# x's block sums of a sparse attention and MoE kernel, cut into ten short steps and built one pass ahead

## The chip, the cores and the metric

The kernel runs on one core of one Trainium2 chip. The metric is the device time of one execution in microseconds (us); before the change it is 1703.1 us, the median of three runs (1699.97 to 1703.55). TensorE multiplies matrices (PE in the profile; its weight loads are PEld), VectorE (DVE) and ScalarE (ACT) do elementwise work, GpSimd (POOL) does elementwise work on SBUF alone, and SyncE (SP) issues all DMAs of this kernel. Each engine works through its own instructions in order; semaphores order the engines among each other.

## The reference

```
scores = q @ k^T / sqrt(64)                 # 4 batches, 8 heads, 576 tokens, 64 columns
heads 0-3: local mask (0 <= i-j < 32);  heads 4-7: strided mask (i >= j, i%32 == j%32)
attn = exp(scores - max) / (sum + 1e-9);    x = attn @ v  as [2304 tokens, 512]
P = exp(x @ w_gate - global max)            # 2304 x 8
8 times: P /= row sum + 1e-9;  P /= column sum + 1e-9;  P *= 2304/8
out = sum over 8 experts e of  P[:, e] * (relu(x @ w1[e]) @ w2[e])      # 512 -> 1024 -> 512
```

All of it is in fp32; every operand of the large products is split into a high part (fp32r, rounded by a copy on ACT) and a low part (source minus high part, a subtraction on POOL or DVE), and a product is three matmuls: high x high, high x low, low x high.

## The kernel before

**Stages.** First comes attention: 32 steps, the first nine ahead of everything else, the rest beside the first expert. Their output x, split in two, lies in `reg`, in five chunks of tokens (four of 512, one of 256), and is also stored to DRAM (`xd`). Second, expert 0 is computed plainly, in 56 *slots* (the loop at L733). A slot is `layer1` of one chunk and one of four blocks of 128 hidden columns (12 matmuls, then ReLU: high part on ACT, low part on DVE), and then `layer2` of the slot before it. The first 36 slots have nine chunks of 256 tokens (first half of the hidden columns, u = 0), the last 20 have the chunks 0, 512, 2048, 1024, 1536 (u = 1), four slots each; the one at 2048 has 256 tokens, the others 512. While attention lasts a slot also has an attention step; from slot 26 on attention is over, and the slots carry other work from generators, one step of each a slot (L754).

Third come experts 1 to 7 in three passes of 768 tokens, 28 groups a pass, 84 in all (the loop at L779). A group (`first`) is seven products of blocks in place of eight, as in Strassen's scheme: hidden blocks come from sums and differences of blocks of w1 (`prep_w1`: three POOL instructions, then four splits) and of x. Its second layer (`second`, six blocks of 12 matmuls) runs inside the next group, as `fill(0)` to `fill(5)`. DVE adds each block times its gate to `acc`.

**The block sums of x.** `build_s(p, k)` makes them for pass p and half k of 256 columns: four loads from `xd` (768 KB in all), on POOL one addition of high and low parts (128x1536) and four differences or sums (128x384), the split (ACT copies 128x1536, POOL subtracts), and two stores to `sd`. The three passes' six builds are one generator `sums()` with three steps a build: loads; POOL's sums; split and stores. All six run in the slots after attention. `st` and `so` have one buffer each.

**The gate.** `gating()` has 28 steps: five times logits and transposes, two for the global maximum, and for each of eight normalizations a row step on DVE (L342 to L347) and a column step (TensorE's sum over partitions with a matrix of ones, L350, then DVE, L352 to L354).

**The first group's operands.** `early()` loads w1 for group 0, prepares it ten slots later, loads w2 and the first three operands of x into `reg`, where chunks no longer needed lay; the other operands of x are loaded behind the slots (L763). After the slots the pools `w1` (four buffers of 4096 bytes a partition) and `h` (two of 4096) are closed, and in their place, in this order, `rab` (12288 bytes: raw w1 blocks and their differences), `u` (4608 bytes: m1, u2, u3) and `hg` are opened (L766). The last slot's layer 2, which reads `h`, runs as `fill(0)` of group 0, behind its first three products (`rest_of_plain`, L774).

**Scaling.** Expert 0's result in `acc` has to be multiplied by its gate before other experts are added. `scale(p)` (L770) does it for six tiles on DVE, in group 0 for the first pass, and behind the last but one group of a pass for the next one (L782).

Of the kernel before, what the change touches and what calls it, by code (L numbers as in the profile page):

```python
# [8 lines left out]
F32 = mybir.dt.float32  # L9
F32R = mybir.dt.float32r  # L10
# [41 lines left out]
def kernel(  # L52
# [9 lines left out]
    nc = tc.nc  # L62
# [91 lines left out]
    def split(hi, lo, src):  # L154
        nc.scalar.activation(hi, src, AF.Copy)  # L155
        nc.gpsimd.tensor_tensor(lo, src, hi.bitcast(F32), op=ALU.subtract)  # L156
# [296 lines left out]
    def build_s(p, k):  # L453

        st = pools["sb"].tile([P, 4, 2, TN], F32, tag="sx", name=f"sx_{p}_{k}", bufs=1)
        t0 = 2 * TN * p
        for i, (dh, th) in enumerate(((0, 0), (0, 1), (1, 1), (1, 0))):
            nc.sync.dma_start(  # L458
                st[:, i], xd[:, :, k + 2 * dh, t0 + TN * th : t0 + TN * (th + 1)]
            )  # L460
        yield
        x, s = st[:, :, 0, :], st[:, :, 1, :]
        nc.gpsimd.tensor_tensor(x, x, s, op=ALU.add)  # L463
        x11, x21, x22, x12 = (x[:, i, :] for i in range(4))
        for i, (a, b, op) in enumerate((
            (x21, x22, ALU.add),
            (x21, x11, ALU.subtract),
            (s[:, 0, :], x11, ALU.subtract),
            (x12, s[:, 2, :], ALU.subtract),
        )):  # L470
            nc.gpsimd.tensor_tensor(s[:, i, :], a, b, op=op)  # L471
        yield
        so = pools["sb"].tile([P, 2, 4, TN], F32R, tag="so", name=f"so_{p}_{k}", bufs=1)
        split(so[:, 0], so[:, 1], s)
        for i in range(2):
            nc.sync.dma_start(sd[:, p, :, i, k, :], so[:, i].bitcast(F32))
        yield

    def load_x(p, name):
        if p >= NPASS:  # L480
            return
        o = xops[name].bitcast(F32)
        if name in SOPS:
            nc.sync.dma_start(o, sd[:, p, SOPS.index(name)])
        else:
            th, dh = int(name[1]) - 1, int(name[2]) - 1
            t0 = 2 * TN * p + TN * th
            nc.sync.dma_start(o, xd[:, :, 2 * dh : 2 * dh + 2, t0 : t0 + TN])

    def load_w1g(g):  # L490
        if g >= NG:
            return
        _, e, j = groups[g]
        pool, tag = (raw_p, "raw") if g == 0 else (pools["rab"], "rab")
        ra, rb = (
            pool.tile([P, 2, 2, P], F32, tag=tag, name=f"r{x}_{g}") for x in ("a", "b")
        )
        for t, i, dh, fh in ((ra, 0, 0, 0), (ra, 1, 1, 1), (rb, 0, 0, 1), (rb, 1, 1, 0)):
            f0 = (FP * fh + j) * P
            nc.sync.dma_start(  # L500
                t[:, i],
                w1[e, 2 * P * dh : 2 * P * (dh + 1), f0 : f0 + P].rearrange("(k p) f -> p k f", p=P),
            )
        wraw[g] = ra, rb

    def load_w2g(g):
        if g >= NG:
            return
        _, e, j = groups[g]
        w2raw[g] = [raw_p.tile([P, D], F32, tag="raw", name=f"r2_{g}_{i}") for i in range(2)]  # L510
        for i in range(2):
            load_w2(w2raw[g][i], e, (FP * i + j) * P)

    def prep_w1(g):

        if g >= NG:
            return
        ra, rb = wraw.pop(g)
        w = wops[g % 2]
        pool, tag = (raw_p, "raw") if g == 0 else (pools["rab"], "rtu")  # L520
        rt, ru = (
            pool.tile([P, 2, 2, P], F32, tag=tag, name=f"r{x}_{g}", bufs=None if g == 0 else 2)
            for x in ("t", "u")
        )
        fl = "p i k f -> p i (k f)"
        a, b, t, u = (x.rearrange(fl) for x in (ra, rb, rt, ru))
        nc.gpsimd.tensor_tensor(  # L527
            t, b[:, 0:1, :].to_broadcast([P, 2, 2 * P]), a, op=ALU.subtract
        )
        nc.gpsimd.tensor_tensor(u[:, 0], a[:, 1], t[:, 0], op=ALU.subtract)  # L530
        nc.gpsimd.tensor_tensor(u[:, 1], b[:, 1], u[:, 0], op=ALU.subtract)
        split(w[:, 0, 0:2], w[:, 1, 0:2], ra)
        yield
        split(w[:, 0, 4:6], w[:, 1, 4:6], ru)
        yield
        split(w[:, 0, 2:4], w[:, 1, 2:4], rt)
        yield
        split(w[:, 0, 6], w[:, 1, 6], rb[:, 1])
        yield
# [121 lines left out]
    def attention_scores():  # L661
        if at_k < NS:
            at_scores(at_k)
# [39 lines left out]
            op=ALU.subtract,  # L703
        )

    def sums():
        for p in range(NPASS):
            for k in range(2):
                yield from build_s(p, k)

    def early():

        load_w1g(0)
        for _ in range(9):
            yield
        yield from prep_w1(0)
        load_w2g(0)
        for name in XOPS[:3]:
            load_x(0, name)

    slots = []
    for u in range(UPE):
# [7 lines left out]
                slots.append((u, c, ft, ci == len(chunks) - 1))  # L730
    bg = []
    prev = None
    for u, c, ft, last in slots:  # L733
        layer1(u, c, ft)
        if last and u + 1 < UPE:
            split_w(u + 1, ft, 0)
        busy = at_k < NS + LAG
        if busy:
            attention_values()
            attention_scores()  # L740
        if prev is not None:
            pu, pc, pft, plast = prev
            layer2(pu, pc, pft)
            if plast and pu + 1 < UPE:
                split_w(pu + 1, pft, 1)
        if busy:
            attention_rest()
            if at_k == NS + LAG:
                store_x()
                stacks["right"].close()  # L750
                pools["sb"] = ctx.enter_context(tc.tile_pool(name="sb", bufs=1, side="right"))
                bg = [gating(), sums()]
        else:
            for x in bg:  # L754
                next(x, None)
            if u == 1 and c[0] == 0 and ft == 0:
                bg.append(early())
        prev = (u, c, ft, last)
    for x in bg:
        for _ in x:  # L760
            pass

    for name in XOPS[3:]:  # L763
        load_x(0, name)
    stacks["left"].close()
    for name, bufs in (("rab", 4), ("u", 1), ("hg", 8)):  # L766
        pools[name] = ctx.enter_context(tc.tile_pool(name=name, bufs=bufs, side="left"))
    load_w1g(1)

    def scale(p):  # L770
        for t in range(6 * p, 6 * (p + 1)):
            nc.vector.tensor_scalar_mul(acc[:, t, :], acc[:, t, :], gate[:, t, 0:1])  # L772

    def rest_of_plain(i):  # L774
        if i == 0:
            layer2(*prev[:3])
            scale(0)

    for g in range(NG):  # L779
        p, e, j = groups[g]  # L780
        first(g, (lambda i: second(g - 1, i)) if g else rest_of_plain)
        if p + 1 < NPASS and e == E - 1 and j == FP - 2:  # L782
            scale(p + 1)
    for i in range(6):
        second(NG - 1, i)

# [78 lines left out]
```

## Time and profile before

| | |
|---|---|
| median of three runs | 1703.1 us (1699.97 to 1703.55) |
| the profiled execution | 1701.88 us, span of its instructions 1699.8 us |
| TensorE busy | 1633.4 us (96%), mean granted clock 0.982 |
| DVE, ACT, POOL busy | 942.0 us (55%), 586.9 us (35%), 958.4 us (56%) |
| TensorE's share of the chain that ended last | 86%; POOL 4%, DMA 3%, DVE 2%, issue 2% |
| DMA | 160.57 MB, mean 94 GB/s |

The profile is of one execution. Busy time counts compute instructions only. The granted clock is TensorE's, as a share of its full 2.4 GHz; a mean below 1 says that the engine ran for part of the stretch at its lower level, 1.2 GHz. The chain that ended last is followed back from the last instruction, at each step to what released it. In a list by time a row has its start, its length, engine, line, operation, what it writes and reads, sizes and a count of merged instructions; in brackets stands how long the engine had been idle before it, and what ended that. A row of matmuls ends with the modelled end of the last, a little behind the start of the next row, so the distance from start to start is what a set of matmuls takes.

### The profile page before, as it was taken

Reading aid. Unit: us, or ns where it says so; the run is one execution under the profiler, and the core shown is the slowest. Engines: PE = TensorE matmul, PEld = TensorE weight load, DVE = VectorE, ACT = ScalarE, POOL = GpSimd, SP = SyncE. Lnnn points to the kernel's source line nnn. Section 1 sums busy time; section 2 is a strip of 40 time slices with the busy share of each in tenths; the row PEclk is TensorE's granted clock in tenths of the full one; section 3 lists DMA queues with packets and bytes.
Section 4 is the critical chain, followed back from the end, with each engine's and each line's share of the span. In section 5 each row is a group of like instructions: output and inputs, shape, how many; then the busy total and the mean of one; then the engine's idle time right before and its main releaser. Section 6 shows DMA issues by size and latency. Waiting matters only on the chain.

```text
span 1699.8 us, 23976 instructions
## 1 busy us (share of the span) xinstructions
PE 1633.4 (96%) x8779; PEld 1446.0 (85%) x8779; DVE 942.0 (55%) x1914; ACT 586.9 (35%) x1386; POOL 958.4 (56%) x862
## 2 busy tenths in 40 slices
PE   6999678889999999999999999999999999999999
PEld 5888556678998998998999899899989989989997
DVE  4664113445566556557556555655665655565565
ACT  6664121113333333333333333333333333333332
POOL 4221464316666665665666666566666666656663
PEclk9999888899999999999999999999999999999999
DMA  6553445422222222224421222222162122222211
GB/s 206 176 165 139 142 164 161 155 69 75 68 57 75 72 64 64 75 69 149 149 69 56 75 72 61 67 75 69 56 242 69 56 75 69 62 68 75 68 51 50
DMA packets 158101, 160.57 MB, mean 94 GB/s; under 512 B 11168, under 2 KB 122272, under 8 KB 157984
## 3 DMA queue, kind: packets, MB, share of 16 engines
q1 hardware_dynamic: 157984, 159.05, 29.7%
q8 instruction: 69, 1.13, 0.3%
q14 instruction: 48, 0.39, 0.1%
HBM read 135.41 MB, written 23.59 MB: 94 GB/s over the span
## 4 chain that ended last, share of the span: by engine, by line
PE 86%; POOL 4%; DMA 3%; DVE 2%; issue 2%; SPq 1%; ACT 1%; POOLq 0%; ACTq 0%; DVEq 0%
PE yg L572 40%; PE bb L555 15%; PE ba L555 10%; PE bc L555 10%; PE y L404 4%; PE ph L380 4%; DMA sx<-xd 2%; POOL sx L471 1%; POOL sx L463 1%; SPq L458 1%; POOL so L156 1%; DVE acc L772 1%; PE tp L257 1%; PE sc L197 1%; PE pv L270 1%
## 5 line engine op out<-in xcount | busy, mean ns | idle before, releaser
L572 PE MATMUL yg<-w2g,h 128*128 128x512 f32 x3024 | 755.8, 394 | 1.4 <-POOL w2g L156 1.2
L572 PEld LDWEIGHTS yg<-w2g,h 128*128 128x128 f32 x3024 | 564.2, 188 | 105.8 <-POOL w2g L156 3.6
L577 DVE SCALAR_TENSOR_TENSOR acc<-yg,gate,acc 128x512 f32<-128x512 f32 x504 | 377.8, 750 | 246.5 <-PE yg L572 246.5
L555 PE MATMUL bb<-reg 128*128 128x384 f32 x1512 | 307.3, 338 | 6.1 <-DVE u L608 6.1
L555 PEld LDWEIGHTS bb<-reg 128*128 128x128 f32 x1512 | 272.0, 188 | 21.8 <-DVE u L608 7.3
L156 POOL TENSOR_TENSOR reg<-rt,reg 128x512 fp32r<-128x512 f32 x84 | 109.1, 1298 | 239.4 <-ACT reg L155 239.4
L156 POOL TENSOR_TENSOR reg<-ru,reg 128x512 fp32r<-128x512 f32 x84 | 120.8, 1438 | 204.1 <-ACT reg L155 199.2
L156 POOL TENSOR_TENSOR w2g<-r,w2g 128x512 fp32r<-128x512 f32 x168 | 217.5, 1295 | 11.2 <-ACT w2g L155 11.2
L555 PE MATMUL ba<-reg 128*128 128x384 f32 x1008 | 205.8, 339 | 0.6 <-ACT m L621 0.6
L555 PE MATMUL bc<-reg 128*128 128x384 f32 x1008 | 203.1, 335 | 0.6 <-POOL reg L156 0.6
L555 PEld LDWEIGHTS ba<-reg 128*128 128x128 f32 x1008 | 182.1, 188 | 15.0 <-ACT m L621 1.0
L611 ACT ACTIVATE h<-u 128x384 fp32r<-128x384 f32 x168 | 88.3, 526 | 270.6 <-DVE u L608 270.6
L555 PEld LDWEIGHTS bc<-reg 128*128 128x128 f32 x1008 | 178.0, 189 | 0.9 <-POOL reg L156 0.9
L608 DVE TENSOR_TENSOR u<-bb,m 128x384 f32<-128x384 f32 x168 | 93.6, 557 | 147.6 <-PE bb L555 137.9
L404 PE MATMUL y<-w,h 128*128 128x512 f32 x432 | 122.3, 428 | 39.7 <-ACT h L386 25.5
L611 ACT ACTIVATE h<-ba 128x384 fp32r<-128x384 f32 x84 | 41.3, 492 | 337.3 <-PE ba L555 337.3
L404 PEld LDWEIGHTS y<-w,h 128*128 128x128 f32 x432 | 84.7, 204 | 61.7 <-ACT h L386 33.6
L527 POOL TENSOR_TENSOR rt<-rb,ra 128x512 f32<-128x512 f32 x84 | 109.3, 1301 | 37.4 <-DMA rb<-in_w 37.4
L156 POOL TENSOR_TENSOR reg<-ra,reg 128x512 fp32r<-128x512 f32 x84 | 108.9, 1296 | 35.6 <-ACT reg L155 35.5
L380 PE MATMUL ph<-reg,w 128*128 128x256 f32 (+1 forms) x672 | 118.4, 327 | 0.0
L608 DVE TENSOR_TENSOR u<-bc,u 128x384 f32<-128x384 f32 x168 | 93.7, 558 | 44.3 <-PE bc L555 41.4
L611 ACT ACTIVATE h<-m 128x384 fp32r<-128x384 f32 x84 | 44.0, 524 | 184.2 <-DVE m L608 184.2
(77 smaller groups left out, 1488.9 us busy)
## 6 DMA issues: line engine op xcount, KB each, us to landing
r<-in_w SPq DMA_DIRECT2D x168, 256.0 KB, 3.1
ra<-in_w SPq DMA_DIRECT2D x168, 128.0 KB, 2.3
rb<-in_w SPq DMA_DIRECT2D x168, 128.0 KB, 2.3
sx<-xd SPq DMA_DIRECT2D x24, 384.0 KB, 5.9
sd<-so SPq DMA_DIRECT2D x12, 768.0 KB, 3.9
reg<-sd SPq DMA_DIRECT2D x12, 768.0 KB, 8.9
xd<-reg SPq DMA_DIRECT2D x4, 2048.0 KB, 8.0
reg<-xd SPq DMA_DIRECT2D x9, 768.0 KB, 8.3
```

The lines of the kernel that those rows point to most:

```text
L156: nc.gpsimd.tensor_tensor(lo, src, hi.bitcast(F32), op=ALU.subtract)
L197: nc.tensor.matmul(sc[QT * j : QT * j + QT, i, :], t[sl, q0 : q0 + QT], t[sl, k0 : k0 + KW], start=True, stop=True,)
L257: nc.tensor.transpose(tp[:nk, i, :rows], sm[:, i0 + i, :], ident[:rows, :rows])
L270: nc.tensor.matmul(pv[DH * j : DH * j + DH, i * QT : (i + 1) * QT], tv[:nk, i, j, :], pt[:nk, i, QT * j : QT * j + QT], start=True, stop=True,
L380: nc.tensor.matmul(ph[:, :n], w[:, i, dt, :], xv(x, dt, c0, n), start=(k == 0), stop=(k == 3 * NDT - 1),)
L404: nc.tensor.matmul(y, h[:, a, i * P : (i + 1) * P], w[:, b, :], start=(ft == 0 and first), stop=(ft == FH - 1 and a == 1),)
L527: nc.gpsimd.tensor_tensor(t, b[:, 0:1, :].to_broadcast([P, 2, 2 * P]), a, op=ALU.subtract)
L555: nc.tensor.matmul(out[:, :TN], w[:, i, k, :], xops[x][:, xi, k, :], start=(start and n == 0), stop=(n == 5), skip_group_check=True,)
L572: nc.tensor.matmul(y, hv[f][:, a, o : o + P], w2s[g][f][:, b, :], start=(n == 0), stop=(n == 5))
L577: nc.vector.scalar_tensor_tensor(acc[:, t, :], y, gate[:, t, e : e + 1], acc[:, t, :], op0=ALU.mult, op1=ALU.add)
L608: nc.vector.tensor_tensor(o, bank, s, op=ALU.add)
L611: nc.scalar.activation(h[i][f][:, 0], src, AF.Relu)
```

## The change

A build is cut into ten steps: loads; the addition in two halves; the four differences in two pairs; an empty step; ACT's copy in two halves; POOL's subtraction in two halves; stores. `sums(p)` makes one pass only. Pass 0 is built in the slots after attention, one step a slot; the sums of pass p + 1 are built in the groups of pass p, one step behind each group. The gate's generator steps twice a slot, behind layer 1 and behind layer 2. `early()` is replaced by a list of work by slot (`beside_second_half`, counted from the first slot of u = 1) which also loads more operands of x and scales the first six tiles of `acc`; all scaling is on ACT, for the next pass two tiles behind each of the first three groups of expert 7. The pool `u` is opened ahead of `rab`.

```diff
--- before.py
+++ after.py
@@ -460,7 +460,11 @@
             )
         yield
         x, s = st[:, :, 0, :], st[:, :, 1, :]
-        nc.gpsimd.tensor_tensor(x, x, s, op=ALU.add)
+        for i in (0, 2):
+            nc.gpsimd.tensor_tensor(
+                x[:, i : i + 2], x[:, i : i + 2], s[:, i : i + 2], op=ALU.add
+            )
+            yield
         x11, x21, x22, x12 = (x[:, i, :] for i in range(4))
         for i, (a, b, op) in enumerate((
             (x21, x22, ALU.add),
@@ -469,9 +473,19 @@
             (x12, s[:, 2, :], ALU.subtract),
         )):
             nc.gpsimd.tensor_tensor(s[:, i, :], a, b, op=op)
-        yield
+            if i % 2:
+                yield
         so = pools["sb"].tile([P, 2, 4, TN], F32R, tag="so", name=f"so_{p}_{k}", bufs=1)
-        split(so[:, 0], so[:, 1], s)
+        yield
+        for i in (0, 2):
+            nc.scalar.activation(so[:, 0, i : i + 2], s[:, i : i + 2], AF.Copy)
+        yield
+        for i in (0, 2):
+            nc.gpsimd.tensor_tensor(
+                so[:, 1, i : i + 2], s[:, i : i + 2], so[:, 0, i : i + 2].bitcast(F32),
+                op=ALU.subtract,
+            )
+            yield
         for i in range(2):
             nc.sync.dma_start(sd[:, p, :, i, k, :], so[:, i].bitcast(F32))
         yield
@@ -703,20 +717,27 @@
             op=ALU.subtract,
         )
 
-    def sums():
-        for p in range(NPASS):
-            for k in range(2):
-                yield from build_s(p, k)
-
-    def early():
-
-        load_w1g(0)
-        for _ in range(9):
-            yield
-        yield from prep_w1(0)
-        load_w2g(0)
-        for name in XOPS[:3]:
-            load_x(0, name)
+    def sums(p):
+        for k in range(2):
+            yield from build_s(p, k)
+
+    def scale(t):
+        nc.scalar.activation(acc[:, t, :], acc[:, t, :], AF.Copy, scale=gate[:, t, 0:1])
+
+    def beside_second_half():
+
+        work = {i: [] for i in range(20)}
+        work[3].append(lambda: load_w1g(0))
+        work[10].append(lambda: load_x(0, "x11"))
+        for i, name in ((12, "s2"), (12, "s1"), (13, "x12"), (16, "s3"), (16, "x22")):
+            work[i].append(lambda name=name: load_x(0, name))
+        w = prep_w1(0)
+        for i in range(5):
+            work[9 + i].append(lambda: next(w, None))
+        work[14].append(lambda: load_w2g(0))
+        for i in range(6):
+            work[14 + i].append(lambda i=i: scale(i))
+        return work
 
     slots = []
     for u in range(UPE):
@@ -730,7 +751,7 @@
                 slots.append((u, c, ft, ci == len(chunks) - 1))
     bg = []
     prev = None
-    for u, c, ft, last in slots:
+    for slot, (u, c, ft, last) in enumerate(slots):
         layer1(u, c, ft)
         if last and u + 1 < UPE:
             split_w(u + 1, ft, 0)
@@ -738,6 +759,8 @@
         if busy:
             attention_values()
             attention_scores()
+        else:
+            next(gat, None)
         if prev is not None:
             pu, pc, pft, plast = prev
             layer2(pu, pc, pft)
@@ -749,38 +772,38 @@
                 store_x()
                 stacks["right"].close()
                 pools["sb"] = ctx.enter_context(tc.tile_pool(name="sb", bufs=1, side="right"))
-                bg = [gating(), sums()]
+                gat, s0 = gating(), sums(0)
+                work = beside_second_half()
         else:
-            for x in bg:
-                next(x, None)
-            if u == 1 and c[0] == 0 and ft == 0:
-                bg.append(early())
+            next(gat, None)
+            next(s0, None)
+            for x in work.get(slot - len(slots) + 20, ()):
+                x()
         prev = (u, c, ft, last)
-    for x in bg:
-        for _ in x:
-            pass
-
-    for name in XOPS[3:]:
-        load_x(0, name)
+    for x in (gat, s0):
+        assert next(x, x) is x
+
+    load_x(0, "s4")
     stacks["left"].close()
-    for name, bufs in (("rab", 4), ("u", 1), ("hg", 8)):
+    for name, bufs in (("u", 1), ("rab", 4), ("hg", 8)):
         pools[name] = ctx.enter_context(tc.tile_pool(name=name, bufs=bufs, side="left"))
     load_w1g(1)
-
-    def scale(p):
-        for t in range(6 * p, 6 * (p + 1)):
-            nc.vector.tensor_scalar_mul(acc[:, t, :], acc[:, t, :], gate[:, t, 0:1])
 
     def rest_of_plain(i):
         if i == 0:
             layer2(*prev[:3])
-            scale(0)
 
     for g in range(NG):
         p, e, j = groups[g]
+        if g % (NG // NPASS) == 0 and p + 1 < NPASS:
+            s0 = sums(p + 1)
         first(g, (lambda i: second(g - 1, i)) if g else rest_of_plain)
-        if p + 1 < NPASS and e == E - 1 and j == FP - 2:
-            scale(p + 1)
+        if p + 1 < NPASS:
+            next(s0, None)
+            if e == E - 1:
+                for i in range(2):
+                    if 2 * j + i < 6:
+                        scale(6 * (p + 1) + 2 * j + i)
     for i in range(6):
         second(NG - 1, i)
```

## Rows read from the trace of the kernel before

**Rows 1.** Stretches: us, busy time (instructions) by engine, PEclk, DMA share, GB/s

```profile
402.00:780.00 378.00, 378.00 (x1879) 340.31 (x1878) 222.22 (x361) 132.02 (x266) 240.02 (x218) 1.00 0.23 68
```

**Rows 2.** Groups, 164 to 361 us: busy us, mean ns | idle before

```profile
L404 PE MATMUL y<-w,h 128*128 128x512 f32 x272 | 78.4, 438 | 39.7 <-ACT h L386 25.5 <-ACT acc L411 7.8 <-DVE acc L413 6.5
...
L387 DVE SCALAR_TENSOR_TENSOR h<-ph,h 128x512 fp32r<-128x512 f32 x16 | 11.0, 690 | 54.2 <-ACT h L386 54.2
...
L387 DVE SCALAR_TENSOR_TENSOR h<-ph,h 128x256 fp32r<-128x256 f32 x14 | 5.9, 423 | 60.1 <-ACT h L386 60.1
...
L343 DVE TENSOR_SCALAR g<-g 128x18 f32<-128x18 f32 x8 | 4.4, 553 | 0.3
...
L322 PE MATMUL pg<-cst,lt 16*128 16x16 f32 x18 | 2.1, 226 | 0.0
```

**Rows 3.** POOL in order of time: builds of sums.

```profile
179.22 3.46 POOL L463 TENSOR_TENSOR sx<-sx 128x1536 f32<-128x1536 f32 x1 [20.75 <-DMA sx<-xd]
...
256.98 3.46 POOL L156 TENSOR_TENSOR so<-sx,so 128x1536 fp32r<-128x1536 f32 x1 [1.59 <-ACT so L155]
272.61 3.50 POOL L463 TENSOR_TENSOR sx<-sx 128x1536 f32<-128x1536 f32 x1 [12.17 <-DMA sx<-xd]
276.19 3.98 POOL L471 TENSOR_TENSOR sx<-sx 128x384 f32<-128x384 f32 x4
```

**Rows 4.** ACT in order of time: copy of one build.

```profile
280.21 1.48 ACT L155 ACTIVATE so<-sx 128x1536 fp32r<-128x1536 f32 x1 [13.94 <-POOL sx L471]
```

**Rows 5.** TensorE in order of time: slots after attention, first groups.

```profile
164.07 1.59 PE L380 MATMUL ph<-reg,w 128*128 128x256 f32 x12
165.50 1.55 PE L404 MATMUL y<-w,h 128*128 128x512 f32 x6
166.89 2.00 PE L313 MATMUL pl<-reg,wgs 128*128 128x512 f32 x8
168.73 1.58 PE L380 MATMUL ph<-reg,w 128*128 128x256 f32 x12
...
282.23 4.79 PE L404 MATMUL y<-w,h 128*128 128x512 f32 x12 [5.20 <-ACT h L386]
...
326.83 0.28 PE L350 MATMUL pc<-g,ones 128*128 128x8 f32 x2
326.97 3.03 PE L380 MATMUL ph<-reg,w 128*128 128x512 f32 x12
329.83 2.95 PE L404 MATMUL y<-w,h 128*128 128x512 f32 x12
332.62 2.95 PE L380 MATMUL ph<-reg,w 128*128 128x512 f32 x12
...
360.99 1.23 PE L555 MATMUL ba<-reg 128*128 128x384 f32 x6
...
384.77 0.72 PE L572 MATMUL yg<-w2g,h 128*128 128x512 f32 x2 [0.96 <-POOL w2g L156]
```

**Rows 6.** DVE in order of time: the gate's row step.

```profile
258.36 2.12 DVE L343 TENSOR_SCALAR g<-g 128x18 f32<-128x18 f32 x1
...
331.60 0.17 DVE L343 TENSOR_SCALAR g<-g 128x18 f32<-128x18 f32 x1
...
332.45 0.43 DVE L347 TENSOR_REDUCE g<-gate 128x8 f32<-128x144 f32 x1
```

**Rows 7.** POOL in order of time: first weights, a steady group.

```profile
363.39 1.29 POOL L527 TENSOR_TENSOR rt<-rb,ra 128x512 f32<-128x512 f32 x1 [37.43 <-DMA rb<-in_w]
...
407.03 1.45 POOL L156 TENSOR_TENSOR reg<-ru,reg 128x512 fp32r<-128x512 f32 x1 [2.38 <-ACT reg L155]
```

**Rows 8.** TensorE in order of time: first pass boundary.

```profile
797.16 1.31 PE L555 MATMUL bb<-reg 128*128 128x384 f32 x6 [0.76 <-DVE u L608]
```

**Rows 9.** ACT in order of time: first copy of group 0.

```profile
367.11 0.49 ACT L621 ACTIVATE m<-ba 128x384 f32<-128x384 f32 x1 [8.11 <-PE y L404]
```

**Rows 10.** SP's queue in order of time: first load into rab.

```profile
358.40 0.90 SPq L500 DMA_DIRECT2D ra<-in_w  x2
```

More of the change, by code (lines that the diff above doesn't have):

```diff
@@ L471, in build_s @@
             nc.gpsimd.tensor_tensor(s[:, i, :], a, b, op=op)
+            if i % 2:
+                yield
+        so = pools["sb"].tile([P, 2, 4, TN], F32R, tag="so", name=f"so_{p}_{k}", bufs=1)
         yield
-        so = pools["sb"].tile([P, 2, 4, TN], F32R, tag="so", name=f"so_{p}_{k}", bufs=1)
-        split(so[:, 0], so[:, 1], s)
+        for i in (0, 2):
[7 more added lines that the diff above has]
+            yield
         for i in range(2):
```

## The prediction

> **What bounds the kernel now.** I read the granted clock and busy time by stretches first, then the groups of instructions between 164 and 361 us, then the order of time there, engine by engine. In the last long stage (84 groups of seven products) TensorE is never idle and has its full clock, 2.4 GHz [rows 1]; only work taken off TensorE could shorten it, and the change takes none. The loss lies ahead of it. Between 164 and 361 us, the slots after attention, TensorE waited 39.7 us in front of layer 2, 25.5 of it for the ReLU on ACT, the rest for accumulations on ACT and DVE behind the same copy [rows 2]. One hole shows how each came about. POOL adds a block of x from 272.61 to 276.11 and then does four differences of 0.99 each to 280.17 [rows 3]. ACT's copy of that block, in its queue since long before, had held ACT for 13.94 us and runs from 280.21 to 281.69 [rows 4]. The ReLU of the next two slots stands behind it, and TensorE starts layer 2 at 282.23 after 5.20 us of nothing; its twelve matmuls then take 4.79 us where others take 2.95 [rows 5], so the clock was at its lower level for part of them. There are six such builds, one hole each.
>
> **How much there is to gain in that stretch.** From the first free slot (164.07) to the first product of the long stage (360.99) is 196.9 us [rows 5]. The work of it at full clock, from start to start of undisturbed rows [rows 5]: layer 1 takes 1.43 us with 256 columns (14 slots) and 2.86 with 512 (16 slots), layer 2 takes 1.39 (15 times) and 2.79 (15 times), four gate products 1.84 and one half as long, eight sums over partitions 0.14, one transpose as much, and all small gate transposes 2.1 [rows 2]. That is 20.0 + 45.8 + 20.9 + 41.9 + 8.3 + 1.3 + 2.1 = 140.3 us. So 56.6 us are lost: the 39.7 of the holes, about 1 at one sum, and some 16 from the lower clock after holes.
>
> **The change, part by part.**
>
> *Six builds become two in this stretch, and ACT's part comes late.* A build is now ten steps, one a slot: loads; two half adds (1.75 each, half of 3.50); two pairs of differences; an empty step; ACT's two half copies; two half subtractions; stores. The first build's loads still land at 179.2 [rows 3], because they start as now; POOL then needs 2 x 1.75 + 3.98 = 7.5 us, to 187. ACT's copies stand in slot 32 (slots counted from 0; 26 is the first free one). Slots 26 to 30 cost 1.43 + 1.39 + 1.84 + 0.4 = 5.1 us each, so slot 32 starts near 192: ACT finds its input ready. The second build loads in slot 36, its copies stand in slot 42, over 30 us later. All six holes go, and the low clock with them: minus 56.6 us, if nothing new is late. The first group's weight step (slots 45 to 49) and the loads of x's blocks keep their order on POOL and SP with some ten slots to spare, so I cost them at nothing.
>
> *What is late next: the gate.* The gate's generator now steps twice in a slot, behind layer 1 and behind layer 2. The product steps are safe: the copy that the transposes need fits beside layer 2. The eight normalizations are not. Today the row step (DVE) and the column step (TensorE's sum) are a slot apart; now only layer 2 lies between. The row step's last reduction ends at 332.88 [rows 6], 3.05 us after layer 2 started at 329.83; layer 2 with 512 columns covers 2.79 of it, so 0.3 us is open. With 256 columns DVE's part of the ReLU is 0.27 us shorter (0.69 against 0.42 [rows 2]) and ACT's, I estimate, by as much for the same columns, some 0.5 together, so the step needs 2.55 us and layer 2 covers 1.39: 1.15 open. The normalizations now fall in slots 32 to 39: four times 1.15, once 1.65 (512 columns, but a short layer 2), three times 0.3, and 0.6 for the maximum in slot 31: 7.8 us. This is the lower bound of the cost.
>
> On top comes POOL. The divisor's small add (L343) takes 0.17 us alone [rows 6], but 2.12 from 258.36 to 260.48 when POOL's subtraction ran from 256.98 to 260.44 [rows 3, 6], and 0.55 in the mean of eight [rows 2]. So a row step is now 0.4 to 0.5 us longer in the mean, unseen because it has a slot. In slots 32 to 36 POOL has eight weight parts of 1.29 and two half subtractions, 13.8 us in about 28, denser than in the stretch where those eight stood; I take 0.8 for five steps and 0.4 for three, 5.2 us. If both sensitive instructions of every step in these slots waited most of a POOL instruction (2 x 0.8), it would be 9.5 us. The Trainium skill (SBUF — State Buffer, section "Who interferes with whom") says why: a VectorE tensor_scalar in its two-port mode, or an instruction with two SBUF inputs, shares a port pair with GpSimd, and the one that comes second waits for the whole instruction of the other. The trace agrees for L343 within 0.04 us; taken for every such instruction the rule gives the 9.5, and shorter POOL steps would limit each wait.
>
> I take 7.8 + 5.2 = 13 us of new waits, each below 4 us. The two levels of the clock enter here too: where such waits take half of a slot, as they may in slots 33 to 35, the clock could fall; the holes above show it after 5 us and more. I put 8 us as the bound for that and 0 in the sum. This part: 56.6 - 13 = 43.6 us gained.
>
> *Into the long stage: four builds, 43.8 us of POOL work (3.50 + 3.98 + 3.46 each), one step behind each group.* A group has 15.7 us. The step enters POOL's queue behind the last weight part of a group and in front of the next group's difference (L527). Two parts later POOL waits 2.38 us for ACT [rows 7] before any part that is needed is late; a step is at most 1.99 us (two differences). So it is covered: 0. Without this cover each of 24 steps would cost up to 2 us (48 us; a gain is excluded, as TensorE has no idle time to give). ACT's two copies (1.48 for the whole, so some 1.65 for both) come four times, the twelve ACT scalings of acc, two behind a group, I estimate at 0.6 each (a third of the columns, and a little). They stand in front of the copy m1, which TensorE needs only three products later: 0, and at most 14 us in all if uncovered. SP issues four loads or two stores behind a group's weight loads; these weights have a whole group until use: 0.
>
> *Scalings leave DVE.* Before a pass boundary six scalings stand on DVE between two groups, and TensorE waits 0.76 us for DVE there [rows 8]. Two boundaries: minus 1.5. Nothing else is late there.
>
> *First group.* Today ACT's copy m1 waits 8.11 us, for layer 2, and runs at 367.11 [rows 9]: the pool u holds m1, and it starts in old layer-1 weights but reaches 512 bytes into the old h tiles, which that layer 2 reads. The pool rab lay wholly in the weights, and its first load went out at 358.40, when layer 1's products were through but not that layer 2 [rows 10]. So a pool waits for all that it overlaps. The new order puts u first, clear of h; but rab behind it now ends 512 bytes inside h (4608 + 12288 against 16384). I expect m1's wait to go and the load of rab to get it. Counted from the group's first product (360.99), layer 2 ends at 6.1. From load to POOL's first difference is 5.0 us (358.40 to 363.39) [rows 7, 10]. Then come POOL's three differences (1.29, and two of half the size, some 2.9 with gaps) and, without pause, six parts (five of 1.29, one of half the size): 7.2. That is 6.1 + 5.0 + 2.9 + 7.2 = 21.2, and the matmuls that need the last part start then; today they start at 384.77, 23.8 after [rows 5]. Minus 2.6. If rab did not wait, m1's wait, DVE's six scalings (3 us) and the slow stretch behind would go fully: minus 6.4. If the longer hole (some 4 us ahead of the second group) costs clock as well: 0.
>
> **Sum.** 43.6 + 0 + 1.5 + 2.6 = 47.7 us off the profiled execution's own 1701.88: 1654.2. That execution lies 1.2 below the median of the three runs (1703.1), inside their spread, so I say 1654.
>
> **The rivals.**
> 1. *The gate's chain stays short and rab does not wait.* For it: the 7.8 us hold with POOL out of the way. Against: POOL's weight parts stand in just those slots. 56.6 - 7.8 + 1.5 + 6.4 = 56.7 gained: 1645.
> 2. *The gate's chain becomes the bound of slots 31 to 39.* DVE waits for POOL at both instructions of every step (17.3 us), and the clock falls (8). For it: L343's 2.12. Against: POOL has pauses between parts. First group at 0: 56.6 - 25.3 + 1.5 = 32.8 gained: 1669.
> 3. *ACT still waits for POOL in both builds left.* Two holes of 6.6 with clock (39.7 + 16 over six, so 9.3 each) stay: 1654 + 19 = 1673. Against: POOL is done 5 us before ACT's step by the count above.
> 4. *The steps surface in the long stage in part*, say 24 times 1 us: 1678. Against: the 2.38 us.
> 5. *The other side: the steps surface whole.* Place: POOL's queue between the last weight part and L527. Price: 43.8 us of POOL, 6.6 of copies, 7.2 of scalings, 57.6 in all, more than the 47.7 gained: 1712, slower by half a per cent. It decides where a step of 2.0 exceeds POOL's 2.38 us of waiting, that is, where this wait turns out not to be free.
>
> **How the numbers follow.** Forecast 0.50 (own range 1648 to 1661); rival 1, 0.20; rival 2, 0.20; rival 3, 0.03; rival 4, 0.05; rival 5, 0.02. The range 1641 to 1669 holds the forecast and most of rivals 1 and 2. About 0.2% (3.4 us) is what a measurement of this kernel tells from no change. All cases but the fifth lie over 1% below: faster 0.97. For no change rivals 4 and 5 would have to meet halfway: 0.01; slower 0.02.
>
> **What would show it.** In the changed profile: no hole in front of layer 2 that ends with ACT's ReLU; the first product of the long stage near 317 us instead of 361; waits of TensorE at the gate's sums for DVE's last reduction, 1 to 3 us each in slots 32 to 36; L343 long where POOL runs; the first load of rab issued only after the last layer 2, and a hole near 4 us ahead of the second group; groups of 15.7 us as before, also where a step runs; no wait at the boundaries. Wrong would be: groups longer than 15.7 us with POOL as what ended the wait, any wait of ACT for POOL's differences before 317 us, or a stretch at the lower clock over all gate slots.

## The result, and the profile after

The changed kernel takes 1658.8 us (median of four runs, 1658.6 to 1659.7) against 1702.6 (four runs beside it), a ratio of 0.975 [0.973, 0.976]. The profiled execution takes 1658.59 us with a span of 1656.8, 43.3 less than the one of before; the forecast was 47.7 less. I divide both executions at three points: the start of slot 26, the first product of the long stage, and the last matmuls of the first second layer's block 0.

| us | before | forecast | after |
|---|---|---|---|
| slot 26 to first product | 196.9 | 153.3 | 159.1 |
| first product to last part of block 0 | 23.8 | 21.2 | 20.4 |
| from there to the span's end | 1315.0 | 1313.5 | 1313.2 |

The remaining 0.3 us lies outside the span. So the stretch after attention fell short by 5.8 us, and the other two came out a little better.

The steady groups first, in stretches of the changed kernel (us, then busy time and instructions of PE, PEld, DVE, ACT and POOL, the granted clock, DMA share, GB/s). This answers to [rows 1]:

```profile
402.00:780.00 378.00, 378.00 (x1879) 340.39 (x1878) 222.67 (x362) 138.21 (x277) 256.64 (x230) 1.00 0.31 97
```

POOL has 16.6 us more to do in it and ACT 6.2, yet TensorE is busy all the time at full clock, as before. Now the groups of instructions from 164 to 323 us of the changed kernel (busy us, mean ns | idle before), to be held against [rows 2]:

```profile
L404 PE MATMUL y<-w,h 128*128 128x512 f32 x272 | 69.6, 400 | 0.0
...
L343 DVE TENSOR_SCALAR g<-g 128x18 f32<-128x18 f32 x8 | 6.3, 782 | 0.3
L345 DVE TENSOR_TENSOR gate<-gate,g 128x144 f32<-128x144 f32 x8 | 4.3, 541 | 0.3
L350 PE MATMUL pc<-g,ones 128*128 128x8 f32 x16 | 3.5, 291 | 11.9 <-DVE g L347 11.7
```

The 39.7 us in front of layer 2 are 0.0. In their place 11.7 us of waiting stand in front of the gate's column sum, for DVE's last reduction of the row step. TensorE in order of time in the changed kernel shows these waits (all but one of 0.16 us) and the matmuls behind them:

```profile
192.62 0.30 PE L334 MATMUL pm<-cst,gb 128*128 128x128 f32 x1 [0.46 <-DVE gb L331]
...
197.98 0.36 PE L350 MATMUL pc<-g,ones 128*128 128x8 f32 x2 [2.23 <-DVE g L347]
198.20 1.67 PE L380 MATMUL ph<-reg,w 128*128 128x256 f32 x12
199.70 1.56 PE L404 MATMUL y<-w,h 128*128 128x512 f32 x6
204.10 0.59 PE L350 MATMUL pc<-g,ones 128*128 128x8 f32 x2 [2.83 <-DVE g L347]
204.54 2.91 PE L380 MATMUL ph<-reg,w 128*128 128x256 f32 x12
...
211.62 0.59 PE L350 MATMUL pc<-g,ones 128*128 128x8 f32 x2 [2.73 <-DVE g L347]
212.07 2.91 PE L380 MATMUL ph<-reg,w 128*128 128x256 f32 x12
214.78 2.76 PE L404 MATMUL y<-w,h 128*128 128x512 f32 x6
218.45 0.39 PE L350 MATMUL pc<-g,ones 128*128 128x8 f32 x2 [0.91 <-DVE g L347]
...
221.56 1.57 PE L404 MATMUL y<-w,h 128*128 128x512 f32 x6
224.65 0.39 PE L350 MATMUL pc<-g,ones 128*128 128x8 f32 x2 [1.52 <-DVE g L347]
...
227.76 2.96 PE L404 MATMUL y<-w,h 128*128 128x512 f32 x12
232.04 0.39 PE L350 MATMUL pc<-g,ones 128*128 128x8 f32 x2 [1.32 <-DVE g L347]
...
323.22 1.23 PE L569 MATMUL ba<-reg 128*128 128x384 f32 x6
...
337.30 1.65 PE L569 MATMUL ba<-reg 128*128 128x384 f32 x4 [2.50 <-POOL reg L156]
...
343.62 0.73 PE L586 MATMUL yg<-w2g,h 128*128 128x512 f32 x2 [0.86 <-POOL w2g L156]
```

Twelve matmuls of layer 1 take 1.67 us at 198.20 and 2.91 at 204.54 and 212.07. The stretches of the changed kernel (columns as above) say why:

```profile
164.00:198.00 34.00, 31.30 (x188) 25.86 (x186) 10.68 (x27) 7.31 (x15) 8.90 (x7) 1.00 0.39 140
198.00:207.00 9.00, 6.17 (x33) 5.55 (x34) 4.88 (x12) 1.53 (x3) 4.33 (x3) 0.83 0.28 87
207.00:219.00 12.00, 8.35 (x32) 6.61 (x31) 7.16 (x16) 3.07 (x6) 6.33 (x5) 0.70 0.68 223
219.00:251.00 32.00, 28.86 (x125) 22.37 (x124) 15.87 (x44) 4.71 (x8) 9.53 (x8) 1.00 0.12 40
```

The granted clock is 0.83 and 0.70 between 198 and 219, so the engine ran for part of that time at 1.2 GHz. All waits of the stretch are 12.2 us (11.7 and 0.46); with the 140.3 us of work that leaves 159.1 - 140.3 - 12.2 = 6.6 us. The lower clock is the larger part of them, but not the whole. Held against like rows at full clock, the two layers 1 of 2.91 us are 1.3 longer each (1.59 in [rows 5]), the layer 2 at 214.78 is 1.2 longer (1.56 at 199.70), and the two sums of 0.59 are 0.2 longer each (0.39 elsewhere): 4.2 us. The granted clock allows little more: 0.17 of 9 us and 0.30 of 12 us are missing, 5.1 us. The other 2.4 us go with the stops themselves, also at full clock: from 221.56 to 227.76 TensorE takes 6.20 us for a layer 2, a sum and a layer 1 that take 1.39 + 0.14 + 2.86 = 4.39 undisturbed, and its wait there is 1.52, so 0.29 is lost beside the wait. (Idle time counts from the modelled end of a row, which lies some 0.15 us behind the start of the next where nothing waits.) With the sum at 238.26, whose row shows no wait but which starts 0.3 us late, there are nine such stops.

On DVE of the changed kernel, the row step of the second normalization and L343 of the seventh, answering to [rows 6]; below, on POOL, what runs beside:

```profile
201.05 1.20 DVE L343 TENSOR_SCALAR g<-g 128x18 f32<-128x18 f32 x1
...
202.58 1.02 DVE L345 TENSOR_TENSOR gate<-gate,g 128x144 f32<-128x144 f32 x1
...
236.91 0.17 DVE L343 TENSOR_SCALAR g<-g 128x18 f32<-128x18 f32 x1
```

```profile
176.10 3.64 POOL L464 TENSOR_TENSOR sx<-sx 128x768 f32<-128x768 f32 x2 [17.62 <-DMA sx<-xd]
179.82 4.06 POOL L475 TENSOR_TENSOR sx<-sx 128x384 f32<-128x384 f32 x4
...
200.94 2.49 POOL L156 TENSOR_TENSOR w<-raw,w 128x512 fp32r<-128x512 f32 x2 [4.23 <-ACT w L155]
...
332.92 1.29 POOL L541 TENSOR_TENSOR rt<-rb,ra 128x512 f32<-128x512 f32 x1 [48.38 <-DMA rb<-in_w]
...
335.98 1.26 POOL L156 TENSOR_TENSOR reg<-ra,reg 128x512 fp32r<-128x512 f32 x1
```

Two weight parts end on POOL near 202.2 and at 203.4. L343 starts 0.1 us after the first and ends at 202.25; L345 ends at 203.60. Each lasts until POOL's instruction beside it is through, within 0.2 us. ACT and SP of the changed kernel, answering to [rows 4, 9, 10]:

```profile
196.28 1.57 ACT L481 ACTIVATE so<-sx 128x768 fp32r<-128x768 f32 x2
...
324.49 0.49 ACT L635 ACTIVATE m<-ba 128x384 f32<-128x384 f32 x1 [2.65 <-PE ba L569]
```

```profile
329.33 0.90 SPq L514 DMA_DIRECT2D ra<-in_w  x2
```

ACT's half copies wait for nothing: POOL was done with the block at 183.9. m1 waits for its own product alone. The first load into `rab` goes out when the last layer 2 is through.

### The profile page after: what moved, and what is told of

Its sections match the earlier page's. It is cut to its first block, busy times and chain, and to the rows that moved or that the text cites. A ratio compares the mean times of both kernels' runs of the same rounds, so it can differ in the third digit from the quotient of the medians.

```text
span 1656.8 us, 23975 instructions
## 1 busy us (share of the span) xinstructions
PE 1622.9 (98%) x8779; PEld 1439.2 (87%) x8779; DVE 929.2 (56%) x1896; ACT 598.1 (36%) x1410; POOL 959.8 (58%) x874
## 4 chain that ended last, share of the span: by engine, by line
PE 93%; DVE 2%; issue 1%; ACT 1%; POOL 1%; DMA 1%; SPq 0%; POOLq 0%; ACTq 0%; DVEq 0%
PE yg L586 41%; PE bb L569 16%; PE ba L569 11%; PE bc L569 10%; PE ph L380 6%; PE y L404 5%; PE tp L257 1%; PE sc L197 1%; PE pv L270 1%; ACT sm L233 1%; PE pl L313 1%; PE sc L214 1%; PE pv L284 0%; POOL reg L156 0%; DVE g L343 0%
## 5 line engine op out<-in xcount | busy, mean ns | idle before, releaser
L404 PE MATMUL y<-w,h 128*128 128x512 f32 x432 | 113.5, 404 | 0.0
L380 PEld LDWEIGHTS ph<-reg,w 128*128 128x128 f32 x672 | 99.2, 196 | 8.8
```

The source lines that it names most:

```text
L380: nc.tensor.matmul(ph[:, :n], w[:, i, dt, :], xv(x, dt, c0, n), start=(k == 0), stop=(k == 3 * NDT - 1),)
L404: nc.tensor.matmul(y, h[:, a, i * P : (i + 1) * P], w[:, b, :], start=(ft == 0 and first), stop=(ft == FH - 1 and a == 1),)
```

## The experiments

Medians are in us, ratios are to the kernel before in the same batch. The last three columns are the three lengths of the table above.

| run | median | ratio | slot 26 to first product | to last part | to the end |
|---|---|---|---|---|---|
| sums alone | 1645.9 | 0.967 [0.965, 0.968] | 140.3 | 24.1 | 1315.1 |
| gate shift | 1647.0 | 0.967 [0.966, 0.968] | 147.0 | 20.3 | 1313.3 |
| pools back | 1657.4 | 0.973 [0.972, 0.975] | 159.1 | 19.3 | 1312.9 |
| rt, ru apart | 1656.5 | 0.973 [0.971, 0.974] | 159.1 | 17.5 | 1313.3 |
| gate once | 1640.6 | 0.964 [0.962, 0.965] | 140.3 | 20.4 | 1313.2 |
| best | 1638.0 | 0.962 [0.961, 0.963] | 140.3 | 17.5 | 1313.2 |
| double steps | 1660.5 | 0.975 [0.974, 0.976] | 161.2 | 20.2 | 1312.8 |
| long steps | 1685.0 | 0.990 [0.988, 0.991] | 178.0 | 20.2 | 1322.4 |
| late ACT | 1678.0 | 0.986 [0.985, 0.988] | 172.6 | 23.8 | 1315.1 |
| no small add | 1652.6 | 0.971 [0.969, 0.972] | 151.0 | 20.3 | 1313.2 |

**The sums alone** (against the kernel before, with `build_s` of the changed one; gate, operands, pools and scaling stay).

```diff
-    def sums():
-        for p in range(NPASS):
-            for k in range(2):
-                yield from build_s(p, k)
+    def sums(p):
+        for k in range(2):
+            yield from build_s(p, k)
...
-                bg = [gating(), sums()]
+                bg = [gating(), sums(0)]
...
+        if g % (NG // NPASS) == 0 and p + 1 < NPASS:
+            s0 = sums(p + 1)
...
+        if p + 1 < NPASS:
+            next(s0, None)
```

> The kernel before with the block sums alone changed (ten short steps, one pass ahead); the gate steps once a slot, the first group's operands, the pools and the scalings stay as before. Theory (the six holes with their slow clock were the loss, and the gate's double step costs some of it back): all 56 us come, since a row step and its column step are a whole slot apart again: 1644 to 1650, below the 1658.8 of the whole change. Rival (the gate and the operands had to move forward for the sums to pay): the stretch behind the slots is late and less than 35 us come: above 1668.

It came as the theory said, and it is 13 us faster than the whole change. Its stretch of free slots, as a row of stretches:

```profile
164.00:304.00 140.00, 140.00 (x705) 116.63 (x704) 52.64 (x122) 28.13 (x53) 40.12 (x31) 1.00 0.36 124
```

TensorE is busy for all of it at full clock, and the stretch is 140.33 us long, the 140.3 that the prediction counted as its work. Behind it the first group has a hole that the kernel before has too (4.60 us at 374.60) and the changed kernel lacks:

```profile
317.91 2.29 PE L569 MATMUL bb<-reg 128*128 128x384 f32 x6 [4.60 <-DVE u L622]
```

**The gate's two steps at other places**: its phase shifted by half a slot, so that the column step comes behind a layer 1 and the row step behind a layer 2 (against the changed kernel, as all that follow unless said).

```diff
-        else:
+        elif slot > 26:
             next(gat, None)
```

> The changed kernel with the gate's steps shifted by half a slot: the first step behind layer 1 of slot 26 is left out, so that each row step (DVE) stands behind layer 2 and its column step (TensorE's sum) behind the next layer 1. Theory (TensorE waits 12.2 us at the sums for the row step, and another 5 to 6 us go to the clock that falls behind the waits): layer 1 of the next slot and layer 2 cover the row step, 1641 to 1644. Rival (the waits are work of DVE that has to be done anyway, and come out again at the ReLU's low part in front of layer 2): 1655 to 1659.

Most of the waits went, and the rival's range was missed by far, but it is 3 us slower than the theory wanted. The gate waits that are left are 0.65, 3.00 and 0.41 us. The 3.00 of this kernel and DVE ahead of it:

```profile
204.04 0.39 PE L350 MATMUL pc<-g,ones 128*128 128x8 f32 x2 [3.00 <-DVE g L347]
204.28 2.34 PE L404 MATMUL y<-w,h 128*128 128x512 f32 x6
```

```profile
199.20 1.25 DVE L354 SCALAR_TENSOR_TENSOR gate<-gate,r 128x144 f32<-128x144 f32 x1
...
200.82 0.82 DVE L343 TENSOR_SCALAR g<-g 128x18 f32<-128x18 f32 x1
...
201.98 1.56 DVE L345 TENSOR_TENSOR gate<-gate,g 128x144 f32<-128x144 f32 x1
```

```profile
199.00 2.62 POOL L156 TENSOR_TENSOR w<-raw,w 128x512 fp32r<-128x512 f32 x2 [2.53 <-ACT w L155]
201.57 1.80 POOL L484 TENSOR_TENSOR so<-sx,so 128x768 fp32r<-128x768 f32 x1
```

Three of DVE's instructions between two sums stand beside POOL's two weight parts and its half subtraction; undisturbed they take 0.31, 0.17 and 0.31. So it is the distance from row step to column step that counts, and with a distance of one layer of 1.4 us it depends on where POOL's parts fall.

**The pools in the old order.**

```diff
-    for name, bufs in (("u", 1), ("rab", 4), ("hg", 8)):
+    for name, bufs in (("rab", 4), ("u", 1), ("hg", 8)):
```

> The changed kernel with the pools in the old order (rab, u, hg). Theory (the wait only changes its owner: m1 or rab's load waits for the last layer 2, and what shortened the first group is that DVE's six scalings left it): the same within 1 us, 1658 to 1660. Rival (the new order gives the 3.4 us of the first group): 1661 to 1663.

It fell just below the range: the old order is about 1 us better than the new one. m1 waits again, and TensorE stops 0.58 us for it and later 1.63 for DVE's `u`, but the first load goes out at 321.53 and the group is 1.1 us shorter.

**rt and ru apart**: the differences in a pool of their own, so that the raw blocks end below the h tiles.

```diff
-    for name, bufs in (("u", 1), ("rab", 4), ("hg", 8)):
+    for name, bufs in (("u", 1), ("rab", 4), ("rtu", 2), ("hg", 8)):
...
-        pool, tag = (raw_p, "raw") if g == 0 else (pools["rab"], "rtu")
+        pool, tag = (raw_p, "raw") if g == 0 else (pools["rtu"], "rtu")
```

> The changed kernel with the two buffers of differences (rt, ru) in a pool of their own behind rab, so that rab lies clear of the old h tiles and only the differences reach into them. Theory (rab's load waits for the last layer 2 because its pool overlaps h by 512 bytes, and POOL's chain behind that load sets the second group): the load goes out some 6 us earlier, the differences start right after layer 2, and 2.5 to 4 us go: 1655 to 1656.5. Rival (the second group is set by ACT's and DVE's chain of the first group): within 0.7 us of 1658.8.

2.2 us less, at the edge of what the theory gave (2.5 to 4). SP and POOL of this kernel:

```profile
321.64 0.90 SPq L514 DMA_DIRECT2D ra<-in_w  x2
```

```profile
330.41 1.29 POOL L541 TENSOR_TENSOR rt<-rb,ra 128x512 f32<-128x512 f32 x1 [44.84 <-DMA r<-in_w]
```

The load now leaves 2.6 us ahead of the first product (324.24 in this kernel), where it left 6.1 behind it, and POOL starts as the last layer 2 ends (the next product is at 330.16), where it started 3.8 us after that (332.92 and 329.14).

**The gate once a slot**, its step only at the end of a slot, and the six scalings of `acc` in the two last slots.

```diff
-            work[14 + i].append(lambda i=i: scale(i))
+            work[18 + i // 3].append(lambda i=i: scale(i))
...
-        else:
-            next(gat, None)
```

> The changed kernel with the gate stepping once a slot, behind layer 2, as before the change; the six scalings of the first pass stand in the last two slots, three in each, since the gate is done only in slot 53. Theory (the gate's double step is the whole of the loss behind the slots, 12.2 us of waits and some 6 of slow clock, and nothing else needs the early gate): the long stage starts near 304.3 us and 18 to 19 us go: 1639 to 1641. Rival (the late scalings hold ACT in front of the first group, or the operands come late): 1644 to 1650.

As expected: the stretch is 140.33 us again and the median 18.2 lower. Nothing else moved (20.4 and 1313.2). The second step a slot is what the whole difference came from.

**Best**: the last two edits together.

> As the kernel with the gate once a slot, and the differences of w1 (rt, ru) in a pool of their own, so that rab does not reach into the old h tiles. Theory (the two losses are independent, 18 to 19 us and 2.2): 1637 to 1639. Rival (the first group is set by something else once the slots before it run without a wait): as with the gate alone.

1638.0 us, 20.8 below the changed kernel: the two gains (18.2 and 2.2) add. It beats both kernels.

**Double steps in the long stage**: for passes 1 and 2 each of the four differences and each half subtraction is issued twice, so that these steps take twice as long.

```diff
-            nc.gpsimd.tensor_tensor(s[:, i, :], a, b, op=op)
+            for _ in range(1 if p == 0 else 2):
+                nc.gpsimd.tensor_tensor(s[:, i, :], a, b, op=op)
...
-            nc.gpsimd.tensor_tensor(
-                so[:, 1, i : i + 2], s[:, i : i + 2], so[:, 0, i : i + 2].bitcast(F32),
-                op=ALU.subtract,
-            )
+            for _ in range(1 if p == 0 else 2):
+                nc.gpsimd.tensor_tensor(
+                    so[:, 1, i : i + 2], s[:, i : i + 2], so[:, 0, i : i + 2].bitcast(F32),
+                    op=ALU.subtract,
+                )
```

> The changed kernel; for the passes built in the long stage every pair of differences and every half subtraction is done twice on POOL (the same values written again), so that 16 of the 24 steps there take 3.5 to 4.0 us in place of 1.75 to 1.99. Theory of the prediction (a step is free up to the 2.38 us for which POOL waits for ACT two parts later): each such step is 1.1 to 1.6 us late for TensorE, 1675 to 1680. Rival (POOL's three pauses of a group, 0.37, 2.38 and 2.85 us, add up, because the first parts behind a step are not needed before the next group): no group is longer, 1658 to 1660.

The rival was right: no group got longer (the median is 1.7 above the changed kernel's, but that lies in the slots after attention, 161.2 against 159.1, where nothing was edited: the waits there come to 11.4 us, 0.8 less than in the changed kernel, but the granted clock is 0.70 over 27 us, from 198 to 225, against 0.76 over 21 us, from 198 to 219, in the changed kernel). POOL around one such step:

```profile
392.68 4.18 POOL L476 TENSOR_TENSOR sx<-sx 128x384 f32<-128x384 f32 x4
...
401.27 1.30 POOL L156 TENSOR_TENSOR reg<-ru,reg 128x512 fp32r<-128x512 f32 x1
...
403.94 1.30 POOL L156 TENSOR_TENSOR reg<-rt,reg 128x512 fp32r<-128x512 f32 x1 [1.37 <-ACT reg L155]
```

The step has eaten the first pause of the group (2.37 at 350.19 of the changed kernel, no step ahead of it) and half of the next (2.84 at 354.48): 4.18 + 1.37 = 5.6 us, near the sum of the two. So POOL may be late by more than the first pause; the numbers fit the sum of its pauses before a part that TensorE waits for.

**Long steps**: `build_s` of the kernel before, three steps a build, under the new order of passes.

> The changed kernel with builds in the three long steps of before (loads; all sums, 7.5 us of POOL; copy, subtraction and stores together), one pass ahead as in the change. Behind the slots two holes of ACT come back, 9.3 us each with the clock, less what the gate's waits shrink by as POOL is done earlier: plus 12 to 19 us there under both theories. In the long stage: theory (the pauses of a group, 5.6 us, cover a step, so a step of 7.5 us costs some 2 us, four times): 1678 to 1686 in all. Rival (one pass ahead is enough, whatever the length of a step, since all its operands are there a group before): no longer group, 1670 to 1678.

The theory was right. POOL and TensorE of this kernel around a build in the long stage:

```profile
378.18 3.52 POOL L463 TENSOR_TENSOR sx<-sx 128x1536 f32<-128x1536 f32 x1
381.78 4.06 POOL L471 TENSOR_TENSOR sx<-sx 128x384 f32<-128x384 f32 x4
```

```profile
393.50 0.97 PE L555 MATMUL bc<-reg 128*128 128x384 f32 x4 [0.24 <-POOL reg L156]
...
396.66 0.74 PE L572 MATMUL yg<-w2g,h 128*128 128x512 f32 x2 [0.96 <-POOL w2g L156]
```

The rest of the run is 9.2 us longer, 2.3 for each of the four builds there; 7.6 us of step less the 5.2 of the two pauses is 2.4. In the slots after attention the copy of the first build holds ACT for 6.07 us, and TensorE waits 4.33 us at a gate transpose behind it; the copy of the second build holds ACT for 8.01 us; the next ReLU stands behind it, DVE's part of that ReLU and the gate's row step behind that, and TensorE waits 12.92 us at the first column sum. So the length of a step matters: 4.2 us are free and 7.6 are not. No length between was run; the two pauses put the point near 5.2, an estimate.

**ACT a slot later, nothing else** (against the kernel before).

```diff
         yield
+        yield
         so = pools["sb"].tile([P, 2, 4, TN], F32R, tag="so", name=f"so_{p}_{k}", bufs=1)
```

> The kernel before with one empty step more in every build, between POOL's sums and ACT's copy; all six builds stay in the slots after attention, in their long instructions. Theory (what held TensorE was ACT standing in its queue in front of POOL's result, not POOL's work): loads and sums take some 16 us from issue, three slots are 11 to 17 us, so most of ACT's wait goes, with most of the slow clock: 1652 to 1668. Rival (six serial builds through one buffer are too much for 30 slots, so they had to leave): less than 20 us come, above 1682.

It lies between what I gave to either side: 24 us of 56 came. One hole on TensorE and its copy on ACT:

```profile
210.76 2.93 PE L404 MATMUL y<-w,h 128*128 128x512 f32 x6 [5.35 <-ACT h L386]
```

```profile
208.96 1.48 ACT L155 ACTIVATE so<-sx 128x1536 fp32r<-128x1536 f32 x1 [8.61 <-POOL sx L471]
```

The copy holds ACT 4 to 10 us a build (13.94 in [rows 4]), and four holes of 2.2 to 6.3 us are left. One slot more is too little for a build of 7.5 us on POOL behind its loads; what the rest took away was builds leaving the stretch and more slots between. These two were not tried apart.

**No small add**: the constant 1e-9 is not added to the row sums.

```diff
-        nc.vector.tensor_scalar_add(g18, g18, 1e-9)
```

> The changed kernel without the small add (1e-9) to the row sums (L343), so the row step has four DVE instructions in place of five; this leaves out that constant. Theory (the row step bounds TensorE in slots 32 to 39, and L343 takes 6.3 us of it, most of that waiting for POOL's weight parts; a part of that wait passes on to L345, the next instruction that waits for POOL): 3 to 6 us go, with some clock: 1652 to 1656. Rival (the wait for POOL passes on whole, as POOL's parts set the pace of these slots): 1657 to 1659.

As expected. TensorE waits 6.5 us at the sums in place of 11.7. Part of the wait for POOL goes on to the next instruction that is open to it (L344 in this kernel is the product with the row factor):

```profile
195.88 1.03 DVE L344 TENSOR_TENSOR gate<-gate,g 128x144 f32<-128x144 f32 x1
```

It takes 1.03 in the first three steps where it takes 0.31 undisturbed. Over all eight steps its excess is 2.8 us, against 1.8 for the same product in the changed kernel, so about 1 us of L343's 4.9 passed on and the rest went. The stretch is 8.1 us shorter: 5.2 are waits, and most of the other 2.9 are clock (0.86 over 12 us, from 198 to 210, and 1.00 before and behind).

## Why the prediction was right, and what it mis-sized

*Six builds become two, ACT's part late: right.* The copies of both builds left wait for nothing, all holes in front of layer 2 are gone, and three kernels with the gate off the path take the 140.33 us that the count of work gave. The 56.6 us were there to be had; rival 3 is out. (A build's four loads are 384 KB each, 1.5 MB in all, twice the figure given above; nothing here rests on it.)

*The gate: the mechanism right, its waits right in sum, what comes with the waits mis-sized.* 13 us of waits were forecast and 12.2 came. The parts differ: the excess of L343 and L345 over 0.17 and 0.31 is 4.9 + 1.8 = 6.7 us where 5.2 was taken for POOL, and what is left, 5.5, stands against 7.8; layer 2 at the lower clock covers more of the chain, which may take back some (not separated). The Trainium skill (SBUF — State Buffer, section "Who interferes with whom") gives the rule that such DVE instructions wait for POOL's whole instruction; the ends of L343 and L345 above agree within 0.2 us.

The term that failed is "8 us as the bound for that and 0 in the sum": the clock cost some 4.2 us, with waits of 2.2, 2.8 and 2.7 us where I looked for 5 and more. Beside it the nine stops lost 2.4 us in all that are no waits, for which the sum had no term. These 6.6 less the 0.8 by which the waits stayed below 13 is the 5.8 us that the stretch came out longer. The once-a-slot run shows that all of it belongs to the gate's second step: without it neither wait nor lower clock is left (TensorE is busy for all of 165 to 305 us, at 1.00). The price of the clock is not the same in every run: with double steps the same slots waited 0.8 us less and still took 2.1 more. With 18.8 us in all the gate stands between the forecast (13) and rival 2 (25.3). The 9.5 us in rival 2's sum do not come out of the terms stated: five steps of 2 x 0.8 are 8.0, which would put rival 2 at 23.8; 18.8 lies below that too.

*Steps in the long stage: 0, right, by a wrong argument.* "It decides where a step of 2.0 exceeds POOL's 2.38 us" was rival 5's point. Steps of 4.2 us cost nothing there, 7.6 us cost 2.3; the cover fits both pauses, 5.2 to 5.6 us.

*Scalings off DVE: right.* 1.5 forecast, 1.8 came; with the scalings kept on DVE the rest of the run was 1315.1, with them on ACT 1312.8 to 1313.3.

*First group: right in size, wrong in what did it.* `rab` took over the wait for the last layer 2 as forecast. 20.4 us came from 6.1 to the load, 3.6 to POOL's first difference (5.0 was taken from [rows 7, 10]), 3.1 and 7.6. But the order of pools was no gain: in the old order, with the scalings on ACT, the group takes 19.3, and with the scalings on DVE 24.1 and 23.8. What gained was DVE's six scalings leaving the group, which I had counted beside m1's wait. In the kernel before they stand in the chain that ended last, on DVE, ahead of the `u` for which TensorE waits 4.60 us at 374.60 (a row of the chain has start, length, engine, what is written and line):

```profile
370.65 2.97 DVE acc L772 x6
```

In the old order without them that wait is 1.63, 3 us less. No run moved the scalings alone. m1's wait cost 0.58. With neither scalings nor `rab`'s wait, in the run with rt and ru apart, the group takes 17.5: minus 6.3, where rival 1 gave 6.4 for that case. Why load to first difference was 1.4 us shorter stays open; with it the hole ahead of the second group, near 4 us among the signs of the forecast, is 2.50 (337.30).

The total of 1654.2 missed 1658.6 by 5.8 - 0.8 - 0.3 - 0.3 = 4.4 us.

## What to carry to other kernels

A change of several parts can hold one that costs: here one generator stepped twice a slot gave back 18 of 57 us, and only undoing parts one at a time showed it. Put producer and consumer on two engines at least one full slot of the pacing engine apart, and count the slot by its shortest form; a tiny DVE instruction beside POOL can take as long as POOL's instruction does (0.17 us alone, 1.20 here). The cover of an in-order engine was here more than its first pause, and near the sum of its pauses up to the first part that someone waits for.

## What the hardware showed that I had not expected

- The granted clock fell behind short waits that follow each other, not only behind long ones: 2.23, 2.83 and 2.73 us with some 3 and then 5 us of work between went with a granted clock of 0.83 and 0.70, while 0.91 to 1.52 us with 5 to 6 us of work between left it at 1.00 (219 to 251 us). In the run without the small add, 1.71 and 1.60 us were followed by one slow layer 2 (2.76 for six matmuls, 1.56 elsewhere).
- Taking away one of two DVE instructions that wait for POOL hands a part of its wait to the other: the two-input product takes 0.31 us when it follows a delayed L343 and no second POOL instruction (217.64 us of the changed kernel), and 1.03 in each of the first three steps without L343.
